# Emitting the second part of an operation plan outside the manual schedule

## Chip, cores and metric

The kernel runs on one core of one Trainium2 chip. The metric is the device time of one execution in microseconds (us); lower is better. Three runs of the kernel before give a median of 821.39 us (818.48 to 822.4).

## What is computed

A batch of eight, with eight heads, 576 tokens and head dimension 64, goes through attention over 32 memory slots. The memory's keys and values are weighted sums of `k` and `v` by a softmax of `phi` over the tokens. The result feeds a two-layer MLP (4608 tokens, 512 to 2048 to 512, squared ReLU), all in float32:

```python
a = softmax(phi, over tokens)                       # b h s m
k_m, v_m = einsum('bhsm,bhsd->bhmd', a, k), einsum('bhsm,bhsd->bhmd', a, v)
attn = softmax(q @ k_m.T / sqrt(64)) @ v_m
x = attn.transpose(0, 2, 1, 3).reshape(4608, 512)
h = x @ w_in
out = (maximum(h, 0) ** 2) @ w_out
```

## The kernel before

Batches are handled in four pairs. The attention weights of a batch stay transposed in two tiles, `ath` (rounded high part) and `atl` (the rest). `v_m` and `w_in` are multiplied once per pair into a tile `vw` (`vw_step`, L689), so that the first MLP product is `attention weights x vw`. Every product is split into high and low parts and added up on PE.

The work on the MLP is cut into 128 **steps** `g`, one for each batch and each of 16 blocks of 128 hidden units. The list `seq` (L370) orders them; step 32 is the first block of batch 2, and so the start of the second pair in the steps. One step is:

- `mm1` (L786): 6 matmuls of 320 columns into PSUM tile `h` (named `h_1`) and 6 of 256 columns (`h_0`), L807; then ReLU into `r` (L811 on ACT or L812 on DVE), its square rounded into `gh` (L813, and L814 for the last 64 tokens into `gl`), the exact square in place (L815 on ACT or L816 on DVE), and the rest `glo` (L817, L818). There are two PSUM buffers for `h`.
- `mm2` (L821): four accumulators `acc`, each with two matmuls from `gh` (L842, L843) and one from `glo` (L845).

In the first half of each later pair (its even batch), `vw_step` runs beside these steps, two per slice `s` of 256 hidden units (`hh` = 0 and 1, named `pvw_s_0` and `pvw_s_1`). Each has 12 matmuls of 256 columns (L698; a row of the trace's order shows them in groups) into **one** PSUM buffer with the tag `pv`. Four casts on ACT (L328, from `copy`) and four subtractions on DVE (L707) then read it into `vw`. The next `pvw` writes the same buffer, so it waits for the fourth subtraction.

The order of everything is made before anything is emitted. Every operation goes into a `Plan` with its costs on the engines that can do it. `order()` (L118) places them by a list schedule with these costs and gives each a planned start, an engine and, on PE, a planned idle time, which `fill` (L350) covers with matmuls of zeros. L977 to L981 then emit all operations sorted by planned start, inside `tc.manual_schedule()`, under which the framework keeps on each engine the order in which the operations were emitted. The framework adds the waits between engines in either case.

Of the kernel before, what the change touches and what calls it, by code (L numbers as in the profile page):

```python
# [31 lines left out]
WAKE = 100  # L32
ROUNDS = 6
FILL = 360.0
BEGIN = {"PE": 1000.0, "DVE": 1100.0, "ACT": 800.0, "POOL": 2100.0, "SP": 800.0}
LEAD = 9000

# [22 lines left out]
class Plan:  # L60
# [21 lines left out]
    def op(self, ways, fn, r=(), w=(), lead=False, cap=None, port=None, size=0):  # L82
        o = Op()
        o.ways, o.fn, o.lead, o.cap, o.port, o.size = ways, fn, lead, cap, port or {}, size
        deps = set()
        for accesses, writing in ((r, False), (w, True)):
            for a in accesses:
                b, key = a if isinstance(a, tuple) else (a, None)
                assert not b.closed, b.slot
                if b.before is not None:  # L90
                    deps.update(b.before.users)
                for k, ops in b.written.items():
                    if key is None or k is None or k == key:
                        deps.update(ops)
                if writing:
                    for k, ops in b.read.items():
                        if key is None or k is None or k == key:
                            deps.update(ops)
        for accesses, writing in ((r, False), (w, True)):
            for a in accesses:  # L100
                b, key = a if isinstance(a, tuple) else (a, None)
                b.users.append(o)
                if writing:
                    if key is None:
                        b.written, b.read = {None: [o]}, {}
                    else:
                        b.written[key] = [o]
                        b.read.pop(key, None)
                else:
                    b.read.setdefault(key, []).append(o)  # L110
        deps.discard(o)
        o.deps, o.users, o.seq = deps, [], len(self.ops)
        for d in deps:
            d.users.append(o)
        self.ops.append(o)
        return o
# [21 lines left out]
    def forward(self, rank):  # L138
        free = dict(BEGIN)
        wire = 0.0  # L140
# [65 lines left out]
    def backward(self, found):  # L206
        last, start, engine, _ = found
        free = {e: 0.0 for e in BEGIN}
        wire = 0.0
# [45 lines left out]
def tt(n):  # L255
    return 68 + 1.04 * n
# [6 lines left out]
def act(n):  # L263
    return 35 + 0.96 * n
# [10 lines left out]
def tile_attention_moe(  # L275
# [41 lines left out]
    plan = Plan()  # L317
# [3 lines left out]
    def st(shape, dt, tag, name, n=1):  # L321
        return plan.buf(tag, lambda slot: sb.tile(shape, dt, tag=slot, name=name, bufs=1), n)

    def pt(tag, name, n=1):
        return plan.buf(tag, lambda slot: ps.tile([P, 512], F32, tag=slot, name=name, bufs=1), n)
# [9 lines left out]
    def vec(ways, fn, r, w, port=BOTH, **more):  # L335
        return op(ways, fn, r=r, w=w, port=port, **more)
# [13 lines left out]
    def fill(n):  # L350

        for _ in range(n):
            if idle is not None and not live:
                nc.tensor.matmul(idle, zero.broadcast_to([P, P]), zero.broadcast_to([P, 512]), start=True, stop=True)
            elif live:
                nc.tensor.matmul(live[min(live)](), zero.broadcast_to([P, P]), zero.broadcast_to([P, 512]), start=False, stop=False)
# [3 lines left out]
                            fill=0.0, base=0, channel_multiplier=1)  # L360
    nc.gpsimd.affine_select(out=bd, in_=bd, pattern=[[32, 4]], compare_op=ALU.is_ge,
                            fill=0.0, base=31, channel_multiplier=-1)
# [420 lines left out]
    def due(g):  # L783
        return (g + 20) * STEP

    def mm1(g):  # L786
        b, ff = seq[g]
        ah, al = att[b]
        V = VW[b, ff // 2]
        c0 = (ff % 2) * P  # L790
        r = st([P, S], F32, "r", f"r{g}", 2)
        gh = st([P, SM], F32R, "gh", f"gh{g}", 2)
        glo = st([P, SM], F32R, "glo", f"glo{g}", 2)
        if ff not in gl or gl[ff][0] != b // 2:
            gl[ff] = b // 2, st([P, 2, 2 * LEFT], F32R, f"gl{ff}", f"gl{g}")
        G = gl[ff][1]
        lc = slice((b % 2) * LEFT, (b % 2 + 1) * LEFT)
        for h in (0, 1):
            cs = TOK[h]
            n = cs.stop - cs.start  # L800
            p = pt("h", f"h{g}_{h}", 2)

            def mm(e, cs=cs, n=n, p=p):
                i = 0
                for l, x in ((0, ah), (0, al), (1, ah)):
                    for hh in (0, 1):
                        nc.tensor.matmul(p()[:, 0:n], V()[:, l, hh, c0:c0 + P], x()[:, hh, cs], start=(i == 0), stop=(i == 5))  # L807
                        i += 1

            op({"PE": 713 if n == 256 else 875}, mm, [V] + [(x, (hh, h)) for x in (ah, al) for hh in (0, 1)], [p])  # L810
            op({"ACT": act(n), **({} if b < 2 else {"DVE": tt(n)})}, lambda e, cs=cs, n=n, p=p: nc.scalar.activation(r()[:, cs], p()[:, 0:n], AF.Relu) if e == "ACT"  # L811
               else nc.vector.tensor_scalar(r()[:, cs], p()[:, 0:n], 0.0, None, ALU.max), [p], [(r, h)])  # L812
        op({"ACT": act(SM)}, lambda e: nc.scalar.activation(gh(), r()[:, 0:SM], AF.Square), [r], [gh])  # L813
        op({"ACT": 148}, lambda e: nc.scalar.activation(G()[:, 0, lc], r()[:, SM:S], AF.Square), [r], [(G, (b % 2, 0))])  # L814
        op({"ACT": act(S), **({} if b < 2 else {"DVE": tt(S)})}, lambda e: nc.scalar.activation(r(), r(), AF.Square) if e == "ACT"  # L815
           else nc.vector.tensor_mul(r(), r(), r()), [r], [r], port=BOTH)  # L816
        vec({"DVE": tt(SM)}, lambda e: nc.vector.tensor_sub(glo(), r()[:, 0:SM], gh().bitcast(F32)), [r, gh], [glo])  # L817
        vec({"DVE": tt(LEFT)}, lambda e: nc.vector.tensor_sub(G()[:, 1, lc], r()[:, SM:S], G()[:, 0, lc].bitcast(F32)), [r, (G, (b % 2, 0))], [(G, (b % 2, 1))])  # L818
        gt[g] = gh, glo

    def mm2(g):  # L821
        b, ff = seq[g]
        f0 = g == 0 or seq[g - 1][0] != b
        f1 = g == len(seq) - 1 or seq[g + 1][0] != b
        gh, glo = gt[g]
        t = wo[ff]
        for i in range(NMAIN):
            if f0:
                acc[i] = pt("acc", f"acc{b}_{ff}_{i}", 4)
        for l in (0, 1):  # L830
            for i in range(NMAIN):
                c = slice(i * P, (i + 1) * P)
                a = acc[i]

                def mm(e, c=c, a=a, l=l, i=i):
                    nonlocal idle
                    idle = None
                    live[i] = a
                    if l == 1 and f1:
                        del live[i]  # L840
                    if l == 0:
                        nc.tensor.matmul(a(), gh()[:, c], t()[:, 0], start=f0, stop=False)  # L842
                        nc.tensor.matmul(a(), gh()[:, c], t()[:, 1], start=False, stop=False)  # L843
                    else:
                        nc.tensor.matmul(a(), glo()[:, c], t()[:, 0], start=False, stop=f1)  # L845

                op({"PE": 235 * (2 - l)}, mm, [glo if l else gh, (t, 0)] + ([] if l else [(t, 1)]), [a], cap=due(g) + 600 * i + 2000 * l)
        if f1:
            home = homes(b) if ff == NFF - 1 else None
            for i in range(NMAIN):  # L850
                if ff < NFF - 1:
                    if i % 2 == 0:
                        part[i // 2] = st([P, 2, DM], F32, f"V{4 + i // 2}", f"part{i // 2}")
                    pp = part[i // 2]
                    op({"ACT": act(DM), "DVE": tt(DM)}, lambda e, i=i, a=acc[i], pp=pp: copy(e, pp()[:, i % 2, :], a()), [acc[i]], [(pp, i % 2)])
                else:
                    ot, x = home[i]
                    evac(acc[i], home[i], lambda ot=ot, x=x: ot()[:, x, :], [(b, 4 * i + c) for c in range(4)], b == 0)
# [43 lines left out]
            dma(store, 32 * n * DM * 4, [home], [], eng="SP" if b >= B - 2 else "POOL")  # L902


    pos = {x: i for i, x in enumerate(seq)}

    def step(g):
        mm1(g)
        mm2(g)
        b, ff = seq[g]  # L910
        if ff == NFF - 1 and b % 2 == (b > 1):
            mm2_left(b | 1, g)
# [46 lines left out]
    for n in range(1, NPAIR):  # L959
# [14 lines left out]
        for ff in range(NFF):  # L974
            step(pos[b1, ff])

    with tc.manual_schedule():  # L977
        for o in plan.order():
            if o.left == "PE":
                fill(int(o.gap / FILL))  # L980
            o.fn(o.left)  # L981


# [28 lines left out]
```

## Time and profile before

| | us |
|---|---|
| median of three runs | 821.39 |
| the profiled execution, its own time | 819.62 |
| its span, first to last instruction | 817.8 |
| PE busy with matmuls in the span | 774.6 |
| DVE busy | 568.8 |
| ACT busy | 368.8 |

PE is the TensorE's matmul stream, PEld its weight loads, which run beside the matmuls. DVE, ACT, POOL and SP are the other engines' in-order queues; SP issues nearly all loads. A row of the timeline has start, duration, engine, line, operation and tiles; a bracket at its end is the engine's idle time ahead of it and what ended it. Numbers of buffers are left out of tile names there, so `h_1` and `h_0` both read `h`, told apart by 320 and 256 columns.

### The profile page before, as it was taken

The numbers are of one execution on the slowest core, as the hardware profiler recorded it, in microseconds if no ns is written. First come the engines' busy times: TensorE is split into PE (matmuls) and PEld (weight loads), VectorE is DVE, ScalarE is ACT, GpSimd is POOL, SyncE is SP. The second block draws the span as 40 slices with busy tenths as digits, with TensorE's granted clock in tenths as the row PEclk, the third lists the DMA queues.
The fourth block names the chain that finished last, engine by engine and source line by source line (L and its number), as shares of the span: only waits on it lengthen the run. The fifth ranks groups of instructions, "written<-read, shape, count | busy, mean of one in ns | idle before, by whom it ended". The sixth has DMA issues, their size and how long they took to land.

```text
span 817.8 us, 13349 instructions
## 1 busy us (share of the span) xinstructions
PE 774.6 (95%) x4944; PEld 645.9 (79%) x4950; DVE 568.8 (70%) x1258; ACT 368.8 (45%) x861; POOL 54.5 (7%) x95
## 2 busy tenths in 40 slices
PE   7799999999999999999999989999999988999994
PEld 4577888978878777888888777888787877888883
DVE  4999979966585666847787656956688565864441
ACT  2588778655543444424334434433434344432220
POOL 4112012201001000000001000010001000000000
PEclk9999999999999999999999999999999999999998
DMA  7988756675634224123464424222415422110001
GB/s 198 319 283 254 242 195 208 210 193 156 156 112 129 85 79 133 32 51 91 129 165 109 128 78 122 66 52 73 129 34 148 116 86 78 29 37 17 1 5 60
DMA packets 91780, 97.89 MB, mean 120 GB/s; under 512 B 23812, under 2 KB 79108, under 8 KB 91716
## 3 DMA queue, kind: packets, MB, share of 16 engines
q1 hardware_dynamic: 82980, 81.55, 34.1%
q0 software_dynamic: 8736, 15.50, 6.5%
q8 instruction: 39, 0.64, 0.3%
q14 instruction: 25, 0.20, 0.1%
HBM read 79.17 MB, written 17.83 MB: 119 GB/s over the span
## 4 chain that ended last, share of the span: by engine, by line
PE 64%; DVE 17%; issue 5%; ACT 5%; DMA 5%; SPq 2%; DVEq 0%; ACTq 0%
PE h L807 16%; PE acc L845 11%; PE acc L842 11%; PE acc L843 10%; PE accl L868 5%; PE pvw L698 4%; DVE vw L707 4%; ACT vw L328 4%; PE pkv L484 2%; DVE glo L817 2%; DVE r L812 2%; PE pvw L679 2%; DMA q<-in_q_dram 1%; PE psc L736 1%; DMA phi<-in_phi_dram 1%
## 5 line engine op out<-in xcount | busy, mean ns | idle before, releaser
L807 PE MATMUL h<-ath,vw 128*128 128x320 f32 (+1 forms) x1024 | 218.3, 300 | 2.6 <-DVE r L812 1.6
L842 PE MATMUL acc<-wo,gh 128*128 128x512 f32 x512 | 210.0, 410 | 0.5 <-ACT gh L813 0.5
L843 PE MATMUL acc<-wo,gh 128*128 128x512 f32 x512 | 201.2, 393 | 0.0
L807 PEld LDWEIGHTS h<-ath,vw 128*128 128x128 f32 x1024 | 171.3, 189 | 20.8 <-DVE r L812 2.9
L845 PE MATMUL acc<-wo,glo 128*128 128x512 f32 x512 | 160.9, 401 | 1.6
L813 ACT ACTIVATE gh<-r 128x512 fp32r<-128x512 f32 x128 | 80.9, 632 | 138.2 <-DVE r L812 129.6
L328 ACT CAST vw<-pvw 64x256 fp32r<-64x256 f32 (+1 forms) x203 | 74.0, 379 | 123.3 <-PE pvw L698 86.3
L707 DVE TENSOR_TENSOR vw<-pvw,vw 64x256 fp32r<-64x256 f32 x192 | 78.7, 420 | 71.9 <-ACT vw L328 70.8
L842 PEld LDWEIGHTS acc<-wo,gh 128*128 128x128 f32 x512 | 96.2, 188 | 24.6 <-ACT gh L813 5.4
L807 PE MATMUL h<-atl,vw 128*128 128x320 f32 (+1 forms) x512 | 109.6, 295 | 0.0
L843 PEld LDWEIGHTS acc<-wo,gh 128*128 128x128 f32 x512 | 96.4, 188 | 16.4
L845 PEld LDWEIGHTS acc<-wo,glo 128*128 128x128 f32 x512 | 89.6, 189 | 20.8 <-DVE glo L817 7.6
L817 DVE TENSOR_TENSOR glo<-r,gh 128x512 fp32r<-128x512 f32 x128 | 87.6, 684 | 9.6 <-ACT r L815 7.5
L811 ACT ACTIVATE r<-h 128x320 f32<-128x320 f32 (+1 forms) x136 | 55.9, 413 | 63.4 <-PE h L807 62.0
L812 DVE TENSOR_SCALAR r<-h 128x256 f32<-128x256 f32 (+1 forms) x120 | 52.6, 447 | 43.6 <-PE h L807 42.6
L807 PEld LDWEIGHTS h<-atl,vw 128*128 128x128 f32 x512 | 82.2, 189 | 0.2 <-DVE atl L774 0.2
L816 DVE TENSOR_TENSOR r<-r 128x576 f32<-128x576 f32 x59 | 44.8, 759 | 30.8 <-ACT gl L814 28.6
L868 PE MATMUL accl<-wo,gl 128*128 128x512 f32 x192 | 53.6, 394 | 0.0
L698 PE MATMUL pvw<-wi,VTh 128*128 128x256 f32 x192 | 37.9, 290 | 15.3 <-PE h L807 8.1
L698 PEld LDWEIGHTS pvw<-wi,VTh 128*128 128x128 f32 x192 | 31.1, 188 | 23.7 <-PE h L807 13.7
L815 ACT ACTIVATE r<-r 128x576 f32<-128x576 f32 x69 | 47.3, 685 | 1.7
L868 PEld LDWEIGHTS accl<-wo,gl 128*128 128x128 f32 x192 | 35.0, 188 | 7.2 <-DVE o L328 0.3
(142 smaller groups left out, 834.8 us busy)
## 6 DMA issues: line engine op xcount, KB each, us to landing
wi<-w_in_hi SPq DMA_DIRECT2D x56, 256.0 KB
wi<-w_in_lo SPq DMA_DIRECT2D x56, 256.0 KB
KV<-in_k_dram SPq DMA_DIRECT2D x32, 256.0 KB
KV<-in_v_dram SPq DMA_DIRECT2D x32, 256.0 KB
raw<-in_moe_w_in_dram SPq DMA_DIRECT2D x16, 512.0 KB
raw<-in_moe_w_out_dram SPq DMA_DIRECT2D x16, 512.0 KB
q<-in_q_dram SPq DMA_DIRECT2D x24, 288.0 KB
out_dram<-o POOLq DMA_DIRECT2D x20, 256.0 KB, 7.9
```

What stands on the lines that cost most here:

```text
L328: nc.scalar.copy(o, i) if e == "ACT" else ENG[e].tensor_copy(o, i)
L698: nc.tensor.matmul(pw()[:, x * SL:(x + 1) * SL], l()[:, 2 * hh + x, :], w(r, x), start=(i == 0), stop=(i == 2))
L707: vec({"DVE": tt(SL)}, lambda e, V=V, pr=pr, src=src: nc.vector.tensor_sub(V()[pr, 1, hh, :], src(), V()[pr, 0, hh, :].bitcast(F32)), [pw, ...
L807: nc.tensor.matmul(p()[:, 0:n], V()[:, l, hh, c0:c0 + P], x()[:, hh, cs], start=(i == 0), stop=(i == 5))
L811: op({"ACT": act(n), **({} if b < 2 else {"DVE": tt(n)})}, lambda e, cs=cs, n=n, p=p: nc.scalar.activation(r()[:, cs], p()[:, 0:n], AF.Rel ...
L812: else nc.vector.tensor_scalar(r()[:, cs], p()[:, 0:n], 0.0, None, ALU.max), [p], [(r, h)])
L813: op({"ACT": act(SM)}, lambda e: nc.scalar.activation(gh(), r()[:, 0:SM], AF.Square), [r], [gh])
L817: vec({"DVE": tt(SM)}, lambda e: nc.vector.tensor_sub(glo(), r()[:, 0:SM], gh().bitcast(F32)), [r, gh], [glo])
L842: nc.tensor.matmul(a(), gh()[:, c], t()[:, 0], start=f0, stop=False)
L843: nc.tensor.matmul(a(), gh()[:, c], t()[:, 1], start=False, stop=False)
L845: nc.tensor.matmul(a(), glo()[:, c], t()[:, 0], start=False, stop=f1)
L868: nc.tensor.matmul(a(), G()[:, l, :], t()[:, w], start=(ff == 0 and n == 0), stop=(ff == NFF - 1 and n == 2))
```

## The change

Operations whose planned start lies ahead of the first operation of step 32 are emitted as before, inside the manual schedule. All others are emitted after that block has been closed, one after the other in the same planned order, each on the engine that the plan chose and with the same zero matmuls ahead of it. There the framework orders the instructions of each engine itself. It takes the order of emission as a priority, and where its own estimate of times says that an instruction would still have to wait, a later one that could run goes first. `mm1`, `mm2`, the tiles, buffers and the planner's numbers stay as they are.

```diff
+STRICT = 32
...
+    firsts = {}
     def step(g):
+        n = len(plan.ops)
         mm1(g)
+        firsts[g] = plan.ops[n]
...
+    def emit(o):
+        if o.left == "PE":
+            fill(int(o.gap / FILL))
+        o.fn(o.left)
+
+    order = plan.order()
+    bound = firsts[STRICT].start
     with tc.manual_schedule():
-        for o in plan.order():
-            if o.left == "PE":
-                fill(int(o.gap / FILL))
-            o.fn(o.left)
+        for o in order:
+            if o.start < bound:
+                emit(o)
+    for o in order:
+        if o.start >= bound:
+            emit(o)
```

No instruction of the computation is added or removed; what differs is their order on each engine, from the point where the trace of before is at about 241 us. Lines behind the new constant stand one or more further down, so that L698, L707, L807, L812 and L845 of before are L699, L708, L808, L813 and L846.

The rows here are the instructions of one engine in order, without times. First PE in the middle of the second pair, at slice 4 (`pvw_4_0` stands a few rows ahead of these). Before:

```order
L845 MATMUL acc_0_1_3137<-wo_1037,glo_3407 128x512
L807 MATMUL h_1_3441<-ath_2933,vw_0_3_3313 128x320 x2
L807 MATMUL h_1_3441<-atl_2935,vw_0_3_3313 128x320 x2
L807 MATMUL h_1_3441<-ath_2933,vw_0_3_3313 128x320 x2
L698 MATMUL pvw_4_1_3449<-wi_4_1_3315,VTh_2343 128x256 x2
L698 MATMUL pvw_4_1_3449<-wi_4_1_3315,VTl_2346 128x256
L698 MATMUL pvw_4_1_3449<-wi_4_1_3315,VTh_2343 128x256 x2
L698 MATMUL pvw_4_1_3449<-wi_4_1_3315,VTl_2346 128x256
L807 MATMUL h_0_3458<-ath_2933,vw_0_3_3313 128x256 x2
```

And in the changed kernel, from the same instruction on:

```order
L846 MATMUL acc_0_1_3138<-wo_1037,glo_3408 128x512
L808 MATMUL h_1_3442<-ath_2933,vw_0_3_3314 128x320 x2
L808 MATMUL h_1_3442<-atl_2935,vw_0_3_3314 128x320 x2
L808 MATMUL h_1_3442<-ath_2933,vw_0_3_3314 128x320 x2
L808 MATMUL h_0_3459<-ath_2933,vw_0_3_3314 128x256 x2
L808 MATMUL h_0_3459<-atl_2935,vw_0_3_3314 128x256 x2
L808 MATMUL h_0_3459<-ath_2933,vw_0_3_3314 128x256 x2
L846 MATMUL acc_0_2_3144<-wo_1037,glo_3408 128x512
L846 MATMUL acc_0_3_3165<-wo_1037,glo_3408 128x512
L808 MATMUL h_1_3477<-ath_2933,vw_0_3_3314 128x320 x2
L699 MATMUL pvw_4_1_3450<-wi_4_1_3316,VTh_2343 128x256 x2
L699 MATMUL pvw_4_1_3450<-wi_4_1_3316,VTl_2346 128x256
```

The six matmuls of `h_0`, two of `acc` and the first two of the next step's `h_1` have moved ahead of `pvw_4_1`; the other four of that `h_1` follow it. The same move stands at slices 3 to 5 of each of the three later pairs, and at slice 6 with a matmul of the scores (`psc`, L736) in place of the two of `h_1`.

DVE at the next slice, where the four subtractions of `pvw_5_0` and of `pvw_5_1` read `pv`. Before:

```order
L707 TENSOR_TENSOR vw_0_5_3537<-pvw_5_0_3528,vw_0_5_3537 64x256
L707 TENSOR_TENSOR vw_1_5_3543<-pvw_5_0_3528,vw_1_5_3543 64x256 x2
L707 TENSOR_TENSOR vw_0_5_3537<-pvw_5_0_3528,vw_0_5_3537 64x256
L812 TENSOR_SCALAR r_3568<-h_1_3553 128x320
L707 TENSOR_TENSOR vw_0_5_3537<-pvw_5_1_3561,vw_0_5_3537 64x256
L812 TENSOR_SCALAR r_3568<-h_0_3570 128x256
L707 TENSOR_TENSOR vw_0_5_3537<-pvw_5_1_3561,vw_0_5_3537 64x256
L707 TENSOR_TENSOR vw_1_5_3543<-pvw_5_1_3561,vw_1_5_3543 64x256 x2
L812 TENSOR_SCALAR r_3610<-h_1_3588 128x320
L812 TENSOR_SCALAR r_3610<-h_0_3602 128x256
L817 TENSOR_TENSOR glo_3617<-r_3568,gh_3596 128x512
```

And in the changed kernel:

```order
L708 TENSOR_TENSOR vw_0_5_3538<-pvw_5_0_3529,vw_0_5_3538 64x256
L708 TENSOR_TENSOR vw_1_5_3544<-pvw_5_0_3529,vw_1_5_3544 64x256
L813 TENSOR_SCALAR r_3569<-h_1_3554 128x320
L708 TENSOR_TENSOR vw_1_5_3544<-pvw_5_0_3529,vw_1_5_3544 64x256
L708 TENSOR_TENSOR vw_0_5_3538<-pvw_5_0_3529,vw_0_5_3538 64x256
L813 TENSOR_SCALAR r_3569<-h_0_3571 128x256
L813 TENSOR_SCALAR r_3611<-h_1_3589 128x320
L708 TENSOR_TENSOR vw_0_5_3538<-pvw_5_1_3562,vw_0_5_3538 64x256
L813 TENSOR_SCALAR r_3611<-h_0_3603 128x256
L818 TENSOR_TENSOR glo_3618<-r_3569,gh_3597 128x512
L708 TENSOR_TENSOR vw_0_5_3538<-pvw_5_1_3562,vw_0_5_3538 64x256
L708 TENSOR_TENSOR vw_1_5_3544<-pvw_5_1_3562,vw_1_5_3544 64x256 x2
```

The ReLU of `h_1` now stands between the second and third subtraction of `pvw_5_0`, and the ReLUs of the next step and a `glo` stand between the subtractions of `pvw_5_1`.

DVE at slice 7, where the scores of the pair's odd batch are worked on as well. Before:

```order
L749 TENSOR_TENSOR S_0_3732<-S_0_3732,red_0_None 128x576
L707 TENSOR_TENSOR vw_0_7_3767<-pvw_7_1_3793,vw_0_7_3767 64x256 x2
L812 TENSOR_SCALAR r_3823<-h_1_3803 128x320
L731 STREAM_TRANSPOSE qT_1_1_3833<-q_1_3728 128x640
L740 STREAM_TRANSPOSE S_1_3838<-psc_1_0_3818 128x256
```

And in the changed kernel:

```order
L750 TENSOR_TENSOR S_0_3733<-S_0_3733,red_0_None 128x576
L813 TENSOR_SCALAR r_3824<-h_1_3804 128x320
L708 TENSOR_TENSOR vw_0_7_3768<-pvw_7_1_3794,vw_0_7_3768 64x256
L753 TENSOR_REDUCE rz_0_None<-S_0_3733 128x18
L708 TENSOR_TENSOR vw_0_7_3768<-pvw_7_1_3794,vw_0_7_3768 64x256
L732 STREAM_TRANSPOSE qT_1_1_3834<-q_1_3729 128x640
```

The ReLU of `h_1` has moved ahead of two subtractions.

Elsewhere: where the second pair begins, one matmul of `h_0` and one of `acc` stand ahead of `pvw_1_0`, and matmuls of the left-over tokens (`accl`, L868) and of `h_1` ahead of `pvw_1_1`; the latter also where the fourth pair begins. On ACT the small square L814 mostly stands ahead of the large one, L813. On SP one load of `k` (tile `KV`) goes ahead of four others at three places, and on POOL stores of the pair before are issued one by one where they were issued in twos. The odd batches' steps, where no `pvw` runs, keep their order on PE but for single matmuls.

## The prediction

> **What bounds the kernel now.** I read the page's busy line and clock first, then PE's waits behind the cut at 241 us, then one period of the regular stretch.
>
> ```profile
> PE 774.6 (95%) x4944; PEld 645.9 (79%) x4950; DVE 568.8 (70%) x1258; ACT 368.8 (45%) x861; POOL 54.5 (7%) x95
> ...
> PEclk9999999999999999999999999999999999999998
> ```
>
> ```profile
> PEld pvw L698 <- PE h L807: 13.7, 11, 1.3
> PEld pvw L698 <- issue: 7.8, 11, 1.5
> PEld acc L845 <- DVE glo L817: 6.7, 12, 0.6
> PEld acc L842 <- ACT gh L813: 5.2, 28, 0.5
> ```
>
> PE is the bound: 95% busy, clock full in every slice. What an order can win are PE's waits. The second fence is the view of waits, weight loads only, from 241 us to the end (us in total, times, longest). Ahead of `pvw` they sum to 13.7 + 7.8 = 21.5 us, ahead of `glo` and `gh` to 6.7 + 5.2 = 11.9 us; together 33.4 us bound any gain from above. (The loads run ahead of the matmuls, so not all of it is lost.)
>
> The regular stretches of the three later pairs, by the view of windows (length, then busy time by engine):
>
> ```profile
> core 0: us, PE busy (x) PEld busy (x) DVE busy (x) ACT busy (x) POOL busy (x), PEclk, DMA share, GB/s
> ...
> 262.48:310.66 48.18, 43.57 (x241) 36.38 (x241) 29.07 (x69) 20.40 (x52) 0.00 (x0) 1.00 0.28 88
> ...
> 452.53:500.64 48.11, 43.58 (x240) 36.35 (x241) 29.06 (x69) 20.33 (x52) 0.00 (x0) 1.00 0.32 100
> 643.09:691.18 48.09, 43.53 (x241) 36.39 (x241) 29.08 (x69) 20.32 (x52) 0.00 (x0) 1.00 0.30 95
> ```
>
> Each holds four periods of two steps, so a period takes 48.1 / 4 = 12.03 us. DVE works 7.3 us of it and ACT 5.1: both have room. One period on PE, from the timeline:
>
> ```profile
> 270.35 0.40 PE L698 MATMUL pvw<-wi,VTh 128*128 128x256 f32 x2
> ...
> 271.07 0.40 PE L842 MATMUL acc<-wo,gh 128*128 128x512 f32 x1
> ...
> 272.00 0.62 PE L845 MATMUL acc<-wo,glo 128*128 128x512 f32 x2
> ...
> 272.45 0.45 PE L807 MATMUL h<-ath,vw 128*128 128x320 f32 x2
> 272.74 0.46 PE L807 MATMUL h<-atl,vw 128*128 128x320 f32 x2
> 273.04 0.46 PE L807 MATMUL h<-ath,vw 128*128 128x320 f32 x2
> ...
> 274.50 0.47 PE L698 MATMUL pvw<-wi,VTh 128*128 128x256 f32 x2 [1.01 <-PE h L807]
> ...
> 275.29 0.40 PE L807 MATMUL h<-ath,vw 128*128 128x256 f32 x2
> ...
> 276.00 0.63 PE L845 MATMUL acc<-wo,glo 128*128 128x512 f32 x2
> ...
> 276.47 0.45 PE L807 MATMUL h<-ath,vw 128*128 128x320 f32 x2
> ```
>
> From start to start, four `acc` matmuls take 272.00 - 271.07 = 0.93 us, six of `h_0` 0.71, two of `h_1` 0.29 (six 0.88), an unhindered `pvw` 0.72. A period has 24, 12, 12 and 12 of them: 5.58 + 1.42 + 1.76 + 1.44 = 10.20 us. So 1.83 us of 12.03 are lost, and most of it in the hole before the second `pvw`: PE could have begun it at 272.45 + 0.88 = 273.33, begins at 274.50, and takes 0.79 instead of 0.72 for it: 1.24 us. Why it waits, ACT and DVE show:
>
> ```profile
> 271.27 0.63 ACT L328 CAST vw<-pvw 64x256 fp32r<-64x256 f32 x2 [2.83 <-PE pvw L698]
> 271.93 0.42 DVE L707 TENSOR_TENSOR vw<-pvw,vw 64x256 fp32r<-64x256 f32 x1 [1.85 <-ACT vw L328]
> 272.38 0.37 ACT L328 CAST vw<-pvw 64x256 fp32r<-64x256 f32 x1 [0.48 <-DVE vw L707]
> 272.79 0.42 DVE L707 TENSOR_TENSOR vw<-pvw,vw 64x256 fp32r<-64x256 f32 x1 [0.43 <-ACT vw L328]
> 273.24 0.37 ACT L328 CAST vw<-pvw 64x256 fp32r<-64x256 f32 x1 [0.48 <-DVE vw L707]
> 273.63 0.77 DVE L707 TENSOR_TENSOR vw<-pvw,vw 64x256 fp32r<-64x256 f32 x2 [0.43 <-ACT vw L328]
> 274.43 0.49 DVE L812 TENSOR_SCALAR r<-h 128x320 f32<-128x320 f32 x1
> ```
>
> Casts and subtractions take turns; the fourth ends at 274.40, and `pvw` starts 0.10 us later. One `pv` buffer, and PE has no other row in front.
>
> **The change, part by part.**
>
> *The regular stretch.* Now `h_0` (0.71), two `acc` (0.46) and two of `h_1` (0.29) stand ahead of the second `pvw`: PE is ready for it at 273.33 + 1.46 = 274.79. On DVE the ReLU of `h_1` stands ahead of the third subtraction; it waits for `h_1`, whose last matmul ends near 273.5, ends at 274.02, and the last two subtractions (0.77) at 274.82. So `pvw` starts at 274.92: 0.13 late plus the 0.07, 0.20 instead of 1.24. **Gain 1.04 us a period.** The four matmuls of `h_1` left behind (0.59) and the next `h_0` (0.71) then run to 277.0.
>
> The ReLU of the first `h_0` follows the subtractions (0.41, to 275.26), and `gh` on ACT ends near 275.9, ahead of the 277.0 at which PE wants it. `glo` is behind the next ReLU (waits for `h_1`, to 276.98), one subtraction and another ReLU, by the means in these rows:
>
> ```profile
> L817 DVE TENSOR_TENSOR glo<-r,gh 128x512 fp32r<-128x512 f32 x128 | 87.6, 684 | 9.6 <-ACT r L815 7.5
> ...
> L812 DVE TENSOR_SCALAR r<-h 128x256 f32<-128x256 f32 (+1 forms) x120 | 52.6, 447 | 43.6 <-PE h L807 42.6
> ```
>
> 276.98 + 0.42 + 0.45 + 0.68 is 278.5 to 278.6. PE reaches it after eight `acc` at 277.0 + 1.86 = 278.86. So the waits for `gh` and `glo`, the other 1.83 - 1.24 = 0.59 us of a period, mostly go; I take 0.45 (bounds: nothing, and all 0.59). The buffer `pv` is free after three more subtractions, at 278.6 + 1.2 = 279.8; the next `pvw` comes at 278.86 + 1.86 = 280.7, a margin of 0.9. Nothing is late next: sum 1.5 us a period.
>
> There are four such holes in each of three pairs, from 274.50 to the one here, 12 in all:
>
> ```profile
> 691.18 0.48 PE L698 MATMUL pvw<-wi,VTh 128*128 128x256 f32 x2 [0.99 <-PE h L807]
> ```
>
> The fourth of a pair leads into the scores' stretch, where DVE is nearly full:
>
> ```profile
> 318.20:341.50 23.30, 22.71 (x123) 19.14 (x123) 21.63 (x49) 10.18 (x25) 0.00 (x0) 1.00 0.31 87
> ```
>
> There I count only 1.04. A pair: 3 x 1.5 + 1.04 = 5.54; three: **16.6 us**.
>
> *Other holes.*
>
> ```profile
> 241.54 0.47 PE L698 MATMUL pvw<-wi,VTh 128*128 128x256 f32 x2 [0.64 <-DVE vw L707]
> ...
> 246.28 0.47 PE L698 MATMUL pvw<-wi,VTh 128*128 128x256 f32 x2 [0.76 <-issue]
> ```
>
> ```profile
> 326.42 0.56 PE L807 MATMUL h<-ath,vw 128*128 128x320 f32 x2 [0.52 <-DVE r L812]
> ```
>
> ```profile
> 627.60 0.47 PE L698 MATMUL pvw<-wi,VTh 128*128 128x256 f32 x2 [1.07 <-issue]
> ```
>
> Ahead of the first stand now one `h_0` matmul and one `acc` (0.12 + 0.23 = 0.35 of 0.64); the second and the last get more rows than they last: 0.35 + 0.76 + 1.07 = **2.2 us**. The third stands once a pair; its ReLU is now ahead of two subtractions (0.77), but DVE has 1.7 us to spare in 23.3: I take half, 3 x 0.26 = **0.8 us**.
>
> *At nothing.* On ACT the small square goes ahead of the large one where that waits for DVE:
>
> ```profile
> 753.01 0.63 ACT L813 ACTIVATE gh<-r 128x512 fp32r<-128x512 f32 x1 [3.26 <-DVE r L812]
> 753.55 0.24 ACT L814 ACTIVATE gl<-r 128x64 fp32r<-128x64 f32 x1
> ```
>
> Its 0.24 us fit into the 3.26; without that cover it would cost 28 x 0.24 = 6.7 us (28 is the count of `gh` waits above). The `k` load moved ahead on SP is one issue of 0.4 us, and the batch it belongs to is needed 11 us on (issue and first use):
>
> ```profile
> 396.61 0.37 SPq L435 DMA_DIRECT2D KV<-in_k_dram  x1
> ```
>
> ```profile
> 407.59 1.41 PE pkv L484 x40
> ```
>
> Stores on POOL have no reader.
>
> *New waits.* Which the new order brings on PE the trace cannot show. Bounds: none, and one like today's for `glo` (6.7 / 12 = 0.56 us) in each of 12 periods, 6.7 us. I take 1.1, nearer to none, since the walk above finds margins everywhere but in the 0.13.
>
> **Sum:** 16.6 + 2.2 + 0.8 - 1.1 = 18.5 us. The profiled execution took 819.62 (span 817.8, and 1.8 around it): 801.1. The median of the runs lies 1.8 above that execution; I put the forecast half of that higher: **802.0**.
>
> **Rivals.**
>
> *Half of it* (0.18). The first-order holes close, but `gh` and `glo` go on waiting and the scores' stretch takes back the fourth: 9 x 1.04 + 2.2 - 1.1 = 10.5 us, 810. For it: DVE is 93% full there. Against: the walk.
>
> *The hole only moves* (0.08): the single buffer's turn sets the period, and whatever is put ahead, `pvw` waits for the same release. Price: none, 820 to 821. Against: two turns of `pvw`, casts and subtractions (270.35 to 274.50, 4.15 us each) need 8.3 of 12.03 us. The Trainium skill, "Perfetto Trace Analysis", section Optimization Strategy, says that the same gap repeating on the engine that should be full can mean too little PSUM for the next tile; read strictly, a new order without a second buffer would gain nothing here, 820 again. The trace agrees with its diagnosis, one buffer and a 1.0 us gap in every period, but the 8.3 us above leave room to fill the gap with other rows.
>
> *Slower* (0.06): DVE's queue becomes the lock. `glo` and two ReLUs now stand between the subtractions of the second `pvw`, each blocking the rest if it waits. It decides where `pv` is released more than 0.9 us later than I walk it; each further us costs one per period. At 3.4 us later, 2.5 us a period are lost against 1.5 won: 12 x 1.0 - 2.2 = 10 us slower, 829.
>
> *All of it* (0.06): every wait above but a fifth goes: 33.4 x 0.8 = 26.7 us, 793.
>
> **How the numbers follow.** The forecast has 0.62. The range, 796 to 812, takes in its bounds (the new waits' 6.7 - 1.1 = 5.6 above, 1.1 below, the 9 x 0.14 = 1.3 of `gh` and `glo` not counted, the rest of the 0.52 holes and the 2 us by which single runs stood off their median) and the half; outside lie the other three, 0.20. A measurement of this kernel tells 0.5%, 4.1 us, from no change. Faster by more: 0.62 + 0.18 + 0.06 = 0.86; same 0.08; slower 0.06.
>
> **What would show it.** A period near 10.5 us between `pvw` of neighbouring slices; waits of PE before `pvw` under 5 us in total behind 241 us; the same order and times ahead of that. Wrong would be holes of 0.5 us and more before L843 or L846 in the regular stretch, or a scores' stretch longer than the 23.3 us.

## The result and the profile after

The changed kernel takes 796.38 us (median of 4 runs, 794.97 to 798.85) against 821.66 us before: a ratio of 0.9703, 95% interval 0.9667 to 0.9738, so 25.3 us less. The forecast was 802.0, its range 796 to 812. The profiled execution after took 794.97 us with a span of 793.2.

The page's busy line and clock after:

```profile
PE 767.0 (97%) x4944; PEld 648.6 (82%) x4950; DVE 570.5 (72%) x1258; ACT 376.8 (48%) x861; POOL 54.7 (7%) x95
...
PEclk9999999999999999999999999999999999999998
```

DVE works as long as before and ACT 8 us longer. PE's 774.6 us are 767.0 now, though it runs the same matmuls: part of a wait counts as busy. A matmul that had to wait for its weights has a longer row (a first one from `gh` 0.50 us in the last rows of this document, 0.40 in the period after, below), and the row ahead of a hole covers the hole's start (in the prediction's period 273.04 + 0.46 = 273.50, where `pvw` could have begun at 273.33).

The view of waits after, weight loads, from 241 us to the end (us in total, times, longest):

```profile
PEld pvw L699 <- issue: 3.7, 16, 0.6
...
PEld acc L843 <- ACT gh L814: 1.8, 4, 0.6
PEld acc L846 <- DVE glo L818: 1.5, 3, 0.5
...
PEld pvw L699 <- PE acc L846: 0.6, 1, 0.6
```

The 21.5 us ahead of `pvw` are 3.7 + 0.6 = 4.3, and the 11.9 us ahead of `gh` and `glo` are 3.3.

For the stages I took as marks the first matmul from `glo` of steps 31, 34, 42, 48 and 63 (and their like in the other pairs). The view of windows, second pair, before:

```profile
235.70:268.40 32.70, 31.05 (x166) 25.91 (x164) 22.80 (x52) 13.84 (x35) 2.69 (x5) 1.00 0.39 125
268.40:316.98 48.58, 44.09 (x244) 37.29 (x245) 29.74 (x70) 20.09 (x52) 0.00 (x0) 1.00 0.28 87
316.98:349.31 32.33, 31.51 (x169) 26.63 (x168) 27.38 (x62) 15.38 (x37) 2.83 (x4) 1.00 0.28 72
349.31:429.09 79.78, 79.61 (x561) 66.06 (x560) 55.02 (x121) 27.86 (x67) 1.49 (x5) 1.00 0.42 111
```

And after, with the regular stretches of the other two pairs:

```profile
235.91:267.68 31.77, 31.05 (x170) 26.46 (x168) 22.81 (x53) 14.05 (x35) 2.70 (x5) 1.00 0.39 128
267.68:309.49 41.81, 41.81 (x241) 36.98 (x242) 29.29 (x68) 20.59 (x52) 0.00 (x0) 1.00 0.33 102
309.49:341.51 32.02, 31.52 (x169) 26.78 (x168) 27.73 (x62) 15.56 (x36) 2.84 (x4) 1.00 0.26 71
341.51:420.80 79.29, 79.26 (x561) 66.08 (x560) 55.80 (x122) 29.40 (x68) 1.49 (x5) 1.00 0.41 111
449.57:491.36 41.79, 41.79 (x241) 36.93 (x242) 29.28 (x68) 20.59 (x52) 0.00 (x0) 1.00 0.33 102
631.75:673.59 41.84, 41.84 (x241) 36.98 (x242) 29.30 (x68) 20.59 (x52) 0.00 (x0) 1.00 0.30 95
```

The second row of each is the regular stretch: 48.58 us before with PE idle for 4.5 of them, 41.81 after with none. It gives 6.77 of the pair's 8.50 us between the marks. At the mark of step 34, though, the two orders are not the same. PE in the changed kernel:

```profile
266.87 0.40 PE L699 MATMUL pvw<-wi,VTh 128*128 128x256 f32 x2
267.10 0.28 PE L699 MATMUL pvw<-wi,VTl 128*128 128x256 f32 x1
267.68 1.20 PE L846 MATMUL acc<-wo,glo 128*128 128x512 f32 x4 [0.30 <-DVE glo L818]
```

Here the first half of `pvw_3_0` (three matmuls, 0.36 us) runs ahead of the mark, in before all of it behind (270.35 in the prediction's period); it is the same in each pair. The last column counts this half in the regular stretch in both kernels. Summed over the three pairs:

| stage | forecast, us | between the marks, us | for the same work, us |
|---|---|---|---|
| entry of the pair | 2.2 | 2.2 | 3.3 |
| regular stretch | 16.6 | 20.2 | 19.1 |
| scores' stretch | 0.8 | 0.6 | 0.6 |
| odd batch | 0 | 1.9 | 1.9 |
| new waits | -1.1 | within the rows above | within the rows above |
| sum | 18.5 | 24.9 | 24.9 |

One period after, from the timeline; first PE, then DVE and ACT:

```profile
283.27 0.63 PE L846 MATMUL acc<-wo,glo 128*128 128x512 f32 x2
283.74 0.45 PE L808 MATMUL h<-ath,vw 128*128 128x320 f32 x2
284.14 0.47 PE L699 MATMUL pvw<-wi,VTh 128*128 128x256 f32 x2
...
286.24 0.40 PE L843 MATMUL acc<-wo,gh 128*128 128x512 f32 x1
...
288.08 0.61 PE L846 MATMUL acc<-wo,glo 128*128 128x512 f32 x2
```

```profile
283.27 0.77 DVE L708 TENSOR_TENSOR vw<-pvw,vw 64x256 fp32r<-64x256 f32 x2
284.07 0.42 DVE L813 TENSOR_SCALAR r<-h 128x256 f32<-128x256 f32 x1
...
286.92 0.67 DVE L818 TENSOR_TENSOR glo<-r,gh 128x512 fp32r<-128x512 f32 x1
287.62 1.30 DVE L708 TENSOR_TENSOR vw<-pvw,vw 64x256 fp32r<-64x256 f32 x3
```

```profile
284.53 0.63 ACT L814 ACTIVATE gh<-r 128x512 fp32r<-128x512 f32 x1 [1.00 <-DVE r L813]
```

PE is ready for `pvw` at 283.74 + 0.29 = 284.03, the fourth subtraction ends at 284.04, `pvw` starts at 284.14. `gh` is done at 285.16, 1.1 us before PE wants it, and `glo` at 287.59, 0.5 us before.

### The profile page after: what moved, and what is told of

It reads as the page before. It is cut to its first block, busy times and chain, and to the rows that moved or that the text cites. A ratio compares the mean times of both kernels' runs of the same rounds, so it can differ in the third digit from the quotient of the medians.

```text
span 793.2 us, 13238 instructions
## 1 busy us (share of the span) xinstructions
PE 767.0 (97%) x4944; PEld 648.6 (82%) x4950; DVE 570.5 (72%) x1258; ACT 376.8 (48%) x861; POOL 54.7 (7%) x95
## 4 chain that ended last, share of the span: by engine, by line
PE 82%; DVE 9%; ACT 3%; DMA 2%; issue 2%; SPq 1%; DVEq 0%; ACTq 0%
PE h L808 22%; PE acc L843 14%; PE acc L846 13%; PE acc L844 13%; PE accl L869 5%; PE pvw L699 5%; PE psc L737 3%; PE pkv L485 2%; PE pvw L680 2%; ACT vw L329 1%; DVE vw L708 1%; DMA raw<-in_moe_w_in_dram 1%; DMA q<-in_q_dram 1%; DVE glo L818 1%; DVE atl L775 1%
## 5 line engine op out<-in xcount | busy, mean ns | idle before, releaser
L808 PE MATMUL h<-ath,vw 128*128 128x320 f32 (+1 forms) x1024 | 216.6, 300 | 1.1 <-DVE atl L651 0.7
L808 PEld LDWEIGHTS h<-ath,vw 128*128 128x128 f32 x1024 | 172.0, 189 | 18.8 <-issue 1.4
L846 PE MATMUL acc<-wo,glo 128*128 128x512 f32 x512 | 159.7, 399 | 0.9 <-DVE glo L818 0.9
L814 ACT ACTIVATE gh<-r 128x512 fp32r<-128x512 f32 x128 | 80.8, 632 | 107.7 <-DVE r L813 99.1
L843 PEld LDWEIGHTS acc<-wo,gh 128*128 128x128 f32 x512 | 96.3, 188 | 21.5 <-ACT gh L814 2.0
L808 PE MATMUL h<-atl,vw 128*128 128x320 f32 (+1 forms) x512 | 110.2, 295 | 0.0
L846 PEld LDWEIGHTS acc<-wo,glo 128*128 128x128 f32 x512 | 90.3, 189 | 16.1 <-DVE glo L818 2.3
L813 DVE TENSOR_SCALAR r<-h 128x256 f32<-128x256 f32 (+1 forms) x120 | 53.8, 448 | 62.7 <-PE h L808 62.0
L708 DVE TENSOR_TENSOR vw<-pvw,vw 64x256 fp32r<-64x256 f32 x192 | 78.4, 418 | 25.7 <-ACT vw L329 22.7
L818 DVE TENSOR_TENSOR glo<-r,gh 128x512 fp32r<-128x512 f32 x128 | 87.8, 686 | 11.1 <-ACT r L816 9.1
L812 ACT ACTIVATE r<-h 128x320 f32<-128x320 f32 (+1 forms) x136 | 55.9, 413 | 62.0 <-PE h L808 61.4
L808 PEld LDWEIGHTS h<-atl,vw 128*128 128x128 f32 x512 | 82.4, 189 | 0.3
L815 ACT ACTIVATE gl<-r 128x64 fp32r<-128x64 f32 x128 | 32.3, 252 | 38.1 <-DVE r L813 36.8
L699 PE MATMUL pvw<-wi,VTh 128*128 128x256 f32 x192 | 37.9, 289 | 0.8 <-issue 0.3
```

The lines of the kernel that those rows point to most:

```text
L699: nc.tensor.matmul(pw()[:, x * SL:(x + 1) * SL], l()[:, 2 * hh + x, :], w(r, x), start=(i == 0), stop=(i == 2))
L708: vec({"DVE": tt(SL)}, lambda e, V=V, pr=pr, src=src: nc.vector.tensor_sub(V()[pr, 1, hh, :], src(), V()[pr, 0, hh, :].bitcast(F32)), [pw, ...
```

## The experiments

The theory: PE's hole, the places of ReLU and `glo` on DVE, and that of `gh` on ACT must change together. The rivals: PE's order alone, the vector engines' order alone, or the way in which the framework sets its waits outside the manual schedule. A period below is from the first `glo` matmul of one even-numbered step to that of the next but one; it is 12.03 before and 10.33 after.

### PE alone, and all but PE

```diff
-    for o in order:
-        if o.start >= bound:
-            emit(o)
+    E = mybir.EngineType
+    with tc.manual_schedule(engines={E.DVE, E.Activation, E.Pool, E.SP}):
+        for o in order:
+            if o.start >= bound:
+                emit(o)
```

This leaves PE alone to the framework (pe_free); with `engines={E.PE}` it is the other way round (pe_fixed).

> Behind the cut only PE is ordered by the framework; DVE, ACT, POOL and SP keep the planned order. PE's rows move as in the change (the second pvw goes behind h_0 and two acc). Theory A (PE's move and the vector engines' move are needed together): in the trace of before, pvw_1 starts at 274.50; with h_0 and two acc (1.17 us) ahead of it PE is ready for it at 273.33 + 1.17 = 274.50, so it starts at the same moment, casts, subtractions, ReLU and gh behind it keep their times, and PE, now ready for gh at 276.81, waits for it until 278.17 as before. The hole moves from pvw to gh: period 12.0, only the holes where the pairs begin go (about 2 us), 819 to 820 us. Theory B (filling PE's hole is the whole gain): 798 to 804 us, period near 10.4.

> Behind the cut PE keeps the planned order; DVE, ACT, POOL and SP are ordered by the framework. Theory A: on DVE the ReLU of h_1 stands ahead of the third subtraction, so pv is released 0.4 us later and the hole ahead of L699 grows from 1.0 to about 1.4 us; 0 to 0.4 us longer a period, 821 to 826 us. Theory C (the gain is in the order of the vector engines and in their fewer wait-only instructions): 798 to 808 us. The odd batches' steps show apart whether their 0.07 us each is from the vector engines' order: 4.53 us a step as before, or 4.46.

**pe_free: 812.47 us**, ratio 0.9891 (0.9863 to 0.9919). **pe_fixed: 826.22 us**, ratio 1.0069 (1.0044 to 1.0095). One move gains 9.4 us and the other loses 4.4, both together gain 25.3. In pe_free the hole ahead of `pvw` is gone and another one stands where a second `h_0` needs the buffer of the first; the timeline of PE and DVE there:

```profile
298.56 0.51 PE L808 MATMUL h<-ath,vw 128*128 128x256 f32 x2 [0.73 <-DVE r L813]
```

```profile
297.76 0.42 DVE L708 TENSOR_TENSOR vw<-pvw,vw 64x256 fp32r<-64x256 f32 x1 [1.34 <-ACT vw L329]
298.10 0.40 DVE L813 TENSOR_SCALAR r<-h 128x256 f32<-128x256 f32 x1
```

The ReLU that frees this buffer stands behind a subtraction that waits for the casts of the very `pvw` that PE has moved back. So the hole did move, as theory A has it, but to `h` and not to `gh`, and it shrank: the period here is 11.61, not 12.0. My walk had `gh` as the next stop and no gain; 9.4 us is more than that, and far from theory B's 20.

pe_fixed behaves as theory A says, 0.2 us above its range. The view of waits, PE, from 240 us:

```profile
PE pvw L699 <- issue: 21.7, 20, 1.4
```

The profile names no releaser here ("issue"), as it did for some of the holes before; by the times it is the fourth subtraction. The hole is 1.43 where it was 1.01, since the ReLU of `h_1` is ahead of the third subtraction; the period is 12.43. It does not have the changed kernel's whole order on DVE: with PE's order planned, the framework leaves `glo` behind the three subtractions (they start at 291.81, `glo` at 294.00).

### A second buffer

```diff
-        pw = pt("pv", f"pvw{n}_{s}_{hh}")
+        tag = "pa.0" if hh == 1 and 3 <= s <= 5 else "pv.0"
+        pw = plan.buf("pv", lambda slot: ps.tile([P, 512], F32, tag=tag, name=f"pvw{n}_{s}_{hh}", bufs=1))
```

In the kernel before (two_pv) every engine's order stays as it was; then the same edit in the changed kernel (two_pv_free).

> The kernel before, manual schedule to the end, every engine's order as it was; only pvw_3_1, pvw_4_1 and pvw_5_1 of each later pair are written into the bank of pa, which stands idle there, so that they do not wait for the subtractions of pvw_k_0. Theory (one pv buffer makes the hole): PE starts the second pvw at 273.33, gh and glo are ready when PE comes to them at 276.8 and 278.7, period 10.3 instead of 12.0 in three of the four periods of a pair: 9 x 1.7 = 15 us less, 805 to 808 us. Rival (DVE's and ACT's chain sets the period, the buffer only shows it): the wait moves to gh L842 and glo L845, 818 to 822 us.

> The changed kernel with the same second buffer. If the new order and the second buffer cure the same hole, only what is left is to be had: a period of 10.33 us against 10.20 of work, 9 x 0.13 = 1.2 us, 794 to 798 us. If a lack of PSUM still costs in the new order: below 790 us.

**two_pv: 808.64 us**, ratio 0.9849 (0.9823 to 0.9875). The period is 10.77 in the slices with the second buffer, 1.25 less than 12.03: the very 1.24 us that the prediction gave the hole. (9 x 1.25 = 11.3 of the 13.2 us; in the profiled execution the part ahead of the second pair, which is unchanged, was 1.3 us shorter.) The rest, the waits for `glo` and `gh`, I had expected to go with it. It stays whole, 10.77 - 10.20 = 0.57 us, as the view of waits, weight loads, shows:

```profile
PEld acc L846 <- DVE glo L818: 6.8, 12, 0.6
PEld acc L843 <- ACT gh L814: 4.7, 25, 0.5
```

So the hole came from the one buffer, and these waits have another cause. It is not shown alone by any run. In before, two_pv and pe_fixed two things go together, `h_0` behind `pvw` on PE and `glo` behind the three subtractions on DVE, and in all three the waits ahead of `glo` are the same (6.7, 6.8 and 6.8 us, 12 times); where both are turned round, in the changed kernel and in hand below, they are gone from these stretches.

**two_pv_free: 800.69 us**, ratio 0.9745 (0.9721 to 0.9769): neither 794 to 798 nor below 790, but 4 us more than the changed kernel alone. Its order shows why. With the buffer free, the framework leaves `pvw` ahead of `h_0`, presumably because it sees no wait there:

```order
L809 MATMUL h_1_3442<-ath_2933,vw_0_3_3314 128x320 x2
L700 MATMUL pvw_4_1_3450<-wi_4_1_3316,VTh_2343 128x256 x2
L700 MATMUL pvw_4_1_3450<-wi_4_1_3316,VTl_2346 128x256
L700 MATMUL pvw_4_1_3450<-wi_4_1_3316,VTh_2343 128x256 x2
L700 MATMUL pvw_4_1_3450<-wi_4_1_3316,VTl_2346 128x256
L809 MATMUL h_0_3459<-ath_2933,vw_0_3_3314 128x256 x2
```

`h_0` then comes 0.72 us later, and so its ReLU and `gh`. The period is 10.73 instead of 10.33, again with waits ahead of `gh` and `glo` (3.8 and 4.5 us in all). On DVE `glo` stands behind the three subtractions again (they start at 300.31, `glo` at 302.49), so the run does not tell the two apart. With the orders that go with each, to put `pvw` later is worth more than to let it run at once.

### The moves made by hand

If order is all, the planned order with a few moves must do the same inside the manual schedule. `kin` holds each `pvw` with its casts and subtractions (`use`, in turns), `c2` is the second `acc` behind the next `h_0`:

```diff
+    order = plan.order()
+    for P_, (n, s, hh, use) in kin.items():
...
+        for o in [P_] + use:
+            order.remove(o)
+        i = order.index(c2) + 1
+        order.insert(i, P_)
+        i = max(i, order.index(GH[g])) + 1 if True else i + 1
+        order[i:i] = use[0:1] + use[2:3] + use[1:2]
+        i += 3
+        i = max(i, order.index(GLO[g]) + 1) if True else i
+        order[i:i] = use[4:5] + use[6:7] + use[3:4] + use[5:6] + use[7:8]
     with tc.manual_schedule():
-        for o in plan.order():
+        for o in order:
```

In hand_glo the last `if True` reads `if False`, so that the last index is not moved behind `GLO[g]`.

> The kernel before, manual schedule to the end, with four moves made by hand at pvw_3_1 to pvw_6_1 of each later pair: on PE the pvw goes behind the next h_0 and two acc; its casts and subtractions go behind the gh of that step on ACT (and so behind the ReLU of h_0 on DVE), the last three subtractions and the last two casts behind its glo. The framework orders nothing. Theory (the gain is these moves on three engines together, whoever makes them): by the rows of before PE reaches gh at 276.8 (ready at 276.0) and glo at 278.7 (ready at 278.8), period 10.3 to 10.5 instead of 12.0, 12 x 1.5 to 1.7: 801 to 804 us. Rival (the framework's mode itself matters, by its waits or semaphores): over 810.

> The same moves, but all four subtractions stay ahead of glo on DVE. Theory: they end at 278.5, two ReLUs follow, and glo is ready at about 280.1 where PE wants it at 278.7: a wait of about 1.4 us ahead of L848 in each period, period 11.7, 12 x 0.3: 815 to 819 us. Rival (DVE has room, the place of glo does not matter): as the hand-made order, 801 to 804.

**hand: 803.68 us**, ratio 0.9791 (0.9759 to 0.9823). Its windows of two periods:

```profile
281.75:291.93 10.18, 10.18 (x61) 9.05 (x60) 6.98 (x18) 4.89 (x15) 0.00 (x0) 1.00 0.32 97
291.93:302.15 10.22, 10.22 (x62) 9.05 (x60) 7.03 (x18) 4.94 (x15) 0.00 (x0) 1.00 0.34 110
```

That is the 10.20 us which the prediction counted as PE's bare work. In these periods the framework's mode adds nothing; it is the order. The ReLU of `h_1` stays behind the first `pvw`'s subtractions here, and `pvw` has no hole: that move of the changed kernel is not needed. The 7 us that are missing against the changed kernel lie outside these periods: the holes at the entries (0.64, 0.79, 1.07) and the odd batches are as before, and the scores' stretch keeps its 0.5 us hole and gets one of 0.65 ahead of a `pvw`.

**hand_glo: 822.15 us**, ratio 1.0027 (1.0004 to 1.0050). With `pvw` moved on PE, `gh` ahead on ACT and the ReLU of `h_0` ahead on DVE, but three more subtractions ahead of `glo`, the whole gain is gone. (The last two casts move too, ahead of ACT's exact square, but that one ends at 292.28, and `glo` starts at 293.39 behind DVE's own work.) Waits of PE from 240 us (L848 is L845 of before):

```profile
PE acc L848 <- DVE glo L820: 17.1, 12, 1.7
```

The mechanism is the expected one, its price 1.68 us a period and not 1.4, so that the period is 12.18 and nothing is left.

### The small square first

In the kernel before, from batch 2 on, ACT's small square (`gl`) is emitted ahead of the large one.

```diff
+    order = plan.order()
+    for o, small in ahead.items():
+        order.remove(small)
+        order.insert(order.index(o), small)
```

> The kernel before, manual schedule to the end; only ACT's order is changed: from batch 2 on the small square (gl) of a step stands ahead of its large one (gh). In the odd batches gl then takes the wait for ACT's own ReLU and gh waits for DVE alone; in the changed kernel gh started 0.04 us behind DVE's ReLU there, before 0.09, and a step took 4.46 us instead of 4.53. Theory (gh's second wait costs that): odd batches 0.5 to 0.75 us shorter each as in the changed kernel, holes at pvw as before: 819 to 821 us, and 0.06 to 0.07 us a step at the end of the fourth pair. Rival (that small gain is from DVE's or PE's order): no step changes, 821 to 822; or gl's 0.24 us delay gh and steps get longer, up to 6.7 us, 828.

**819.02 us**, ratio 0.9981 (0.9964 to 0.9998). In the fourth pair's odd batch each step is 0.06 to 0.07 us shorter, 0.65 us in all, where the changed kernel has 0.76; over the three odd batches it is 1.2 of 1.9 us. The timeline of before, and then of gl_first, DVE's ReLU and the `gh` that follows it on ACT:

```profile
757.03 0.42 DVE L812 TENSOR_SCALAR r<-h 128x256 f32<-128x256 f32 x1 [1.58 <-PE h L807]
757.54 0.63 ACT L813 ACTIVATE gh<-r 128x512 fp32r<-128x512 f32 x1 [3.27 <-DVE r L812]
```

```profile
754.05 0.42 DVE L813 TENSOR_SCALAR r<-h 128x256 f32<-128x256 f32 x1 [1.70 <-PE h L808]
754.51 0.63 ACT L814 ACTIVATE gh<-r 128x512 fp32r<-128x512 f32 x1 [2.83 <-DVE r L813]
```

`gh` starts 0.09 us behind the ReLU's end in the first and 0.04 in the second. In the built program of before, `gh` has two waits, for ACT's own ReLU and, as an instruction of its own ahead of it, for DVE's; with `gl` ahead, `gl` takes the wait for ACT's ReLU and the extra instruction is gone. In pe_fixed the odd steps shorten as well (0.06 us each), in pe_free hardly (0.14 us over the whole batch). So this part of the gain, 1.2 us, is ACT's order; the other 0.7 us of the odd batches stay open.

### Where the cut stands

Only `STRICT` changes: 64, 16, 0, and no manual schedule at all (s_all).

> The changed kernel with the cut at step 64, the start of the third pair: the second keeps the planned order. Theory (each pair's gain is its own): of the 24.9 us that the changed kernel's PE gains behind its cut the second pair's 8.5 stay away, 16.4 us less than before: 804 to 806 us. Rival (the first freed pair pays for the passage from one order to the other, or the pairs shift each other): off by over 2 us.

> The changed kernel with the cut at step 16 instead of 32. Between 75 us and 241 us its PE waits only once for more than 0.1 us (1.06 at 171.3). Theory: same time as the changed kernel, 795 to 797 us. Rival: the framework's order also shortens waits of the weight loads that no hole shows, 793.

> The cut at step 0, near 44 us. From there to 241 us PE's holes sum to about 3.3 us in the changed kernel, most of them behind DVE or ACT chains of the memory and attention of the first pair. Theory: at most half of them go, 794 to 797 us. Rival: the planner's long view is worth more in the first pair, where loads and decoding compete, and an order by the framework's nearer view loses there: 798 to 805.

> No manual schedule at all, the plan gives only the order of emission. PE's holes ahead of 45 us sum to about 8 us in the changed kernel and end with loads (DMA) and DVE's chain. Theory: loads set these, nothing to win, 794 to 798. Rival: loads and decoding get out of step and the start becomes longer: over 800.

| cut | us | ratio, 95% interval |
|---|---|---|
| 64 | 805.05 | 0.9815 (0.9790 to 0.9840) |
| 32, the change | 796.38 | 0.9703 (0.9667 to 0.9738) |
| 16 | 796.09 | 0.9694 (0.9665 to 0.9724) |
| 0 | 807.54 | 0.9832 (0.9795 to 0.9869) |
| none | 811.10 | 0.9875 (0.9811 to 0.9940) |

Cut 64 takes the second pair's 8.5 us away and nothing else: the pairs' gains add up. Cut 16 changes nothing, as expected. Cut 0 costs 11 us, more than I allowed its rival: the later pairs still gain, but the last step of the first pair comes 11.1 us later than in the changed kernel. Waits of PE there, in the run with cut 0 (37 to 247 us) and then in the changed kernel (37 to 236):

```profile
PE h L808 <- ACT r L812: 3.5, 3, 1.9
PE pmx L473 <- DVE mc L472: 2.2, 1, 2.2
```

```profile
PE pmx L473 <- DVE mc L472: 1.1, 1, 1.1
...
PE h L808 <- ACT r L812: 0.2, 1, 0.2
```

In the first pair, with decoding and loads beside the steps, the planner's order is the better one. PE's idle time there is 10.5 us against 4.2, so that idle time explains 6 of the 11 us. The granted clock explains some of the rest: from 60 to 80 us it is 0.91 in the run with cut 0 and 1.00 in the changed kernel, by estimate 0.09 x 20 = 1.8 us. Which orders on ACT and DVE cause the idle time, and where the last 3 us come from, I did not take apart. Without any manual schedule the four executions took 804.64 to 816.64 us, and their mean clock fell in the same order from 0.988 to 0.975, so that row's time is in part the clock. No order tried beats the changed kernel by more than the measurement can tell.

## Why the prediction was right, and where it fell short

**The hole.** Predicted: 0.20 us left of 1.24 in each period. Left, by the rows of the period after: 0.11 ahead of `pvw` and 0.08 in its first matmuls, 0.19. The fourth subtraction was to end 0.03 us behind PE's readiness and ended 0.01 behind it. The gain of 1.04 stands, and two_pv, which removes the hole by a buffer alone, measures its full size at 1.25.

**`gh` and `glo`.** The mis-sized term. I took 0.45 us a period of at most 0.59, and nothing in the period that leads into the scores' stretch. The period fell by 1.70, so that with the hole's 1.05 all of it went, 0.65 by this count, and the period into the scores gave 1.3 instead of 1.04. A pair: 3 x 1.70 + 1.3 = 6.4 instead of 5.54 (6.77 between the marks, with the half of `pvw_3_0` that moved across one). The walk itself had shown margins of 1.1 us for `gh` and 0.3 for `glo`; after that there was no ground to hold a quarter back.

**Other holes.** For the same work 3.3 measured for 2.2; that the marks give 2.2 is chance. The second pair's entry gave 1.3 for 1.1 and the fourth's 1.1 for 1.07. The third's gave 1.0 where I counted nothing: it shows no hole in PE's rows, but two waits of the weight loads ahead of `pvw`, 1.1 us together, that are gone after. Scores' stretch: 0.6 for 0.8, and it is no longer than before (32.02 against 32.33), so DVE's 93% did not take the gain back.

**At nothing.** Wrong by 1.9 us. The small square ahead of the large one was charged against a wait that hides it; it does not cost but gains, 1.2 us by the second wait that it takes from `gh` (gl_first); the cause of the other 0.7 is open. Such a wait does not stand in the order of rows.

**New waits.** The -1.1 was not needed: those that PE now has are 0.2 to 0.3 us each and lie within the stages' rows. The margin of `pv` towards the next `pvw`, predicted as 0.9, is 1.0 (the subtractions end at 288.92, `pvw` starts at 289.90).

**Rivals.** *The hole only moves* is what happens when PE alone is freed (11.61), and *slower* when DVE and ACT are (12.43), or when subtractions stand ahead of `glo` (12.18). Both mechanisms exist; that all three engines move together is what kept them out. For *half of it* the waits for `gh` and `glo` would have had to stay and the scores' stretch to grow. *All of it*, which I gave 0.06, came nearest: its 793 is 3.4 us from the 796.38 measured and the forecast 5.6, and of the 33.4 us of waits ahead of `pvw`, `gh` and `glo` 25.8 went, where it said 26.7. The result lies only 0.4 us inside the range, since the terms for the regular stretch, the entries and the odd batches were all too small and the charge for new waits was not needed. The Trainium skill's rule ("Perfetto Trace Analysis", Optimization Strategy) that a repeating gap can mean too little PSUM names a true cause here, by two_pv's 1.25 us a period. But the second buffer without the moves leaves 808.64, the moves without the buffer 796.38, and both 800.69.

A slip in the section on the kernel: one `pvw` has 6 matmuls of 256 columns, and 12 is the count of a period, as the prediction's sum has it.

## What to carry to other kernels

When a hole on the full engine ends with a buffer's release, ask not only how to release it earlier but which rows can stand in front of it; those rows then run earlier, and what they feed gets slack as well. Such a move pays only if the queues behind it move along: an in-order engine that holds a needed operation behind one that waits for the moved work gives the gain back, wholly in hand_glo. A planner's order and the framework's can each be the better in different stages of one kernel, so try the border between them.

## What the runs showed that I had not expected

- In gl_first's pair of rows the ACT operation with two waits starts 0.09 us after the later releaser's end, the one with a single wait 0.04 us; per step on the path 0.06 to 0.07 us.
- A wait of PE costs more than its gap. In two_pv a gap of 0.1 us ahead of `gh` is followed by a first matmul that takes 0.33 us from start to start, where it takes 0.23 without one. Its weight load starts only 0.01 us ahead of it there, and 0.12 ahead in the changed kernel (286.12 and 286.24).

The second from the timeline of two_pv, PE and then PEld:

```profile
275.31 0.40 PE L808 MATMUL h<-ath,vw 128*128 128x256 f32 x2
275.66 0.50 PE L843 MATMUL acc<-wo,gh 128*128 128x512 f32 x1
275.99 0.39 PE L844 MATMUL acc<-wo,gh 128*128 128x512 f32 x1
276.22 0.40 PE L843 MATMUL acc<-wo,gh 128*128 128x512 f32 x1
```

```profile
275.65 0.19 PEld L843 LDWEIGHTS acc<-wo,gh 128*128 128x128 f32 x1 [0.15 <-ACT gh L814]
275.76 0.19 PEld L844 LDWEIGHTS acc<-wo,gh 128*128 128x128 f32 x1
```
